# Attention and SwiGLU block on one core: order of batch 1, ends of the output tiles, and the place of the gate/value units changed

## The chip, the cores and the metric

The kernel runs on one core of one Trainium2 chip. The time is the device time of that core in microseconds (us); less is better. Three runs of the kernel before took 422.85, 424.26 and 424.94 us, so their median is 424.26 us.

## What is computed

Attention with 16 extra "beacon" keys, for 8 batches of 8 heads, 576 queries of 64 elements each, and then a SwiGLU block over all 4608 tokens, from 512 to 1536 and back to 512 columns:

```
B, H, S, Nb, D = (8, 8, 576, 16, 64)
k_all = np.concatenate([beacon_k, k], axis=2)
v_all = np.concatenate([beacon_v, v], axis=2)
scores = scale * np.matmul(q, k_all.transpose(0, 1, 3, 2))
causal[:, Nb:] = np.triu(np.ones((S, S), dtype=bool), k=1)
scores = np.where(causal, -1000000000.0, scores)
scores = scores - scores.max(-1, keepdims=True)
a = np.exp(scores)
a /= a.sum(-1, keepdims=True) + 1e-09
return np.matmul(a, v_all).astype(np.float32)
...
x = np.ascontiguousarray(attn_out.transpose(0, 2, 1, 3)).reshape(B * S, H * D)
...
g = x @ w_gate
silu = g * (1.0 / (1.0 + np.exp(-g)))
val = x @ w_val
return (silu * val @ w_out).astype(np.float32)
```

## The kernel before

The code writes out the order of every engine by hand (`manual_schedule`, line 83): each engine and each DMA queue runs its instructions in program order, and an instruction whose operand isn't ready holds all that stand behind it on its engine.

**Work pieces.** Attention is worked through in steps (b, m): batch b, pair of heads m = 0 to 3. A step has

- `scores1` and `scores2` (lines 245 to 249, by `scores`, line 210): matmuls of qT and kT into the PSUM tiles s_ps, two exponentials on ACT each, and selects for the causal mask on POOL; whatever loads wait in `pool_todo` are issued on POOL behind them;
- `pv` (line 253), once for each head of the pair *before*: 15 matmuls into pv_ps, a reciprocal and a multiply on DVE that write x.

The SwiGLU block runs over chunks of 512 tokens. Chunk j has 12 units `G()` (`gv_unit`, line 326): eight matmuls into gv_ps with the gate and value weights, a tanh on ACT, and two DVE operations (u, then hT). Its output is four tiles of 128 tokens; each takes 12 matmuls into o_ps, one for each unit of the chunk, then one DVE copy to o_sb and one DMA to the output on the queue of SP (`out_steps`, line 330). `F(n)` issues the next n of these output matmuls, so a call of `F` can end one tile and begin the next. Units wait in the list `gq`, output matmuls in `fq`; `G()` and `F(n)` do nothing where their list is empty.

**PSUM.** `big` holds three buffers of two banks that s_ps and gv_ps share in turn; `att` and `outp` are one bank each (lines 79 to 81). pv_ps sits in att. Output tiles of chunks 0 to 5 sit in outp alone (`one_bank`), as do the transposes of batch 1; later chunks alternate between outp and att (`two_banks`). So a new tile in outp waits until DVE has copied the tile before it.

**Where operands come from.** Batches 0 and 1 load q and k as fp32; `cast_k` (DVE) and `cast_q` (ACT for batch 1) make them bf16, and `transpose_k`, `transpose_q` turn one pair of heads on TensorE (five matmuls into outp, one DVE copy each). Batches 2 to 7 have q and k transposed by DMA: `dma_transposes(b)` (line 195) is a list of ten DMAs on the queue of SP, column blocks 0 to 4, k then q in each. `scores1` reads column blocks 0 to 4 of qT (the columns 112 to 575 in its second pair of matmuls). x is turned into xT by TensorE for batches 0 and 1 (`x_transpose_pair`, line 277) and by five or six DMAs on the queue of SP for later batches (`x_transpose`, line 285). The queue of SP therefore carries, in program order, the output DMAs, the transposes of q and k, and the transposes of x.

**The order around the change.** Lines 450 to 471 are batch 1: four steps with one unit of chunk 0 in each, then the rest. Lines 472 to 483 are a run of all 12 units of chunk 1, with one transpose of batch 2 behind each. Lines 486 to 517 are the main loop, steps (2,0) to (7,3), each of them

```
G()
scores1(b, m)
if prev:
    pv(*prev, 0)
F(n)
scores2(b, m)
G()
...
    pv(*prev, 1)
F(n)
```

followed by another `G()` and by up to four transposes of the next batch. Chunk b-1 is put into `gq` at the end of step (b,1), for b > 2; chunk b-2 into `fq` in the middle of step (b,1), for b > 3. Lines 518 to 538 are the tail: the last `pv`, the rest of chunk 6, chunks 7 and 8, and the last output tiles.

Of the kernel before, what the change touches and what calls it, by code (L numbers as in the profile page):

```python
# [36 lines left out]
def p_slice(t, q):  # L37

    if t == 0:
        return (0, 16 + q) if q < 496 else (1, 336 + q - 496)  # L40
    if t == 1:
        return 0, 512 + q - 112
    return 1, {2: -240, 3: 512 - 368, 4: 416 - 480}[t] + q
# [3 lines left out]
def kernel(  # L47
# [19 lines left out]
    NF = DFF // P  # L67
# [13 lines left out]
    outp = ctx.enter_context(tc.tile_pool(name="outp", bufs=1, space=bass.MemoryType.PSUM))  # L81
# [20 lines left out]
    def tiles(t):  # L102
        return t[:].rearrange("p (c h d) -> p c h d", c=NKT, h=H)
# [64 lines left out]
    def cast_k(b, m):  # L168
        d, t, h = tiles(kb[b % 2]), tiles(k32), slice(2 * m, 2 * m + 2)
        nc.vector.tensor_copy(d[:, 0:4, h, :], t[:, 0:4, h, :])  # L170
        return nc.vector.tensor_copy(d[0:80, 4, h, :], t[0:80, 4, h, :])

    def cast_q(b, m):
        d, t, h = tiles(qb[b % 2]), tiles(q32), slice(2 * m, 2 * m + 2)
        for o, i in ((d[:, 0:4, h, :], t[:, 0:4, h, :]), (d[0:64, 4, h, :], t[0:64, 4, h, :])):
            if b:
                nc.scalar.activation(o, i, ACT.Copy)
            else:
                nc.vector.tensor_copy(o, i)

    def transpose_pair(dst, src, n, b, m, pool, tag):
        t_ps = pool.tile([P, KPAD], BF16, name="t_ps", tag=tag)
        t, h = tiles(src[b % 2]), slice(2 * m, 2 * m + 2)
        for c in range(NKT):
            r = P if c < 4 else n
            nc.tensor.transpose(t_ps[:, P * c : P * c + r], t[0:r, c, h, :], ident[0:r, 0:r])  # L186
        nc.vector.tensor_copy(dst[b % 2][:, m, 0 : 4 * P + n], t_ps[:, 0 : 4 * P + n])  # L187

    def transpose_k(b, m, pool, tag):
        transpose_pair(kT, kb, 80, b, m, pool, tag)  # L190

    def transpose_q(b, m, pool, tag):
        transpose_pair(qT, qb, 64, b, m, pool, tag)
# [16 lines left out]
    def scores(b, m, which, spec, cols):  # L210
        s = [big.tile([P, 1024], FP32, name="s_ps", tag="big") for _ in range(2)]
        for t, col, q0, n in spec:
            for hh in range(2):
                r = slice(64 * hh, 64 * hh + 64)
                nc.tensor.matmul(  # L215
                    s[hh][:, col : col + n],
                    lhsT=kT[b % 2][r, m, P * t : P * t + P],
                    rhs=qT[b % 2][r, m, q0 : q0 + n],
                    start=True,
                    stop=True,  # L220
                )
        for hh in range(2):
            p = pt[2 * (m % 2) + hh][which]
            nc.scalar.activation(  # L224
                p[:, cols[0] : cols[1]], s[hh][:, cols[0] : cols[1]], ACT.Exp, scale=0.125
            )

            both = p[:].rearrange("p (a j) -> p a j", a=2)[:, :, 0:P]
            selects = [(both, [[0, 2], [1, P]], 0)]
            if which:  # L230
                selects.append((p[:, 416:512], [[1, 96]], -16))
            for ap, pattern, base in selects:
                nc.gpsimd.affine_select(  # L233
                    out=ap,
                    in_=ap,
                    compare_op=ALU.is_ge,
                    fill=0.0,
                    base=base,
                    pattern=pattern,
                    channel_multiplier=-1,  # L240
                )
        for load in pool_todo.pop(0) if pool_todo else []:
            load()
# [4 lines left out]
    def scores2(b, m):  # L248
        scores(b, m, 1, SCORES2, P2_COLS)
# [3 lines left out]
    def pv(b, m, hh):  # L253
        h = 2 * m + hh
        if h == 0:
            xs[b] = x_pool.tile([P, NKT, DM], BF16, name="x")
        o_ps = att.tile([P, NKT, 68], FP32, name="pv_ps", tag="att")
        for c, (q0, _) in enumerate(QBLOCKS):
            for t in range(c + 1):
                w, col = p_slice(t, q0)  # L260
                nc.tensor.matmul(  # L261
                    o_ps[:, c, 0 : D + 1],
                    lhsT=pt[2 * (m % 2) + hh][w][:, col : col + P],
                    rhs=vb[b % 2][:, t, h, 0 : D + 1],
                    start=(t == 0),
                    stop=(t == c),
                )
        rec = rec_pool.tile([P, NKT, 1], FP32, name="rec")
        nc.vector.reciprocal(rec[:], o_ps[:, :, D : D + 1])  # L269
        nc.vector.tensor_tensor(  # L270
            out=xs[b][:, :, D * h : D * h + D],
            in0=o_ps[:, :, 0:D],
            in1=rec[:].to_broadcast([P, NKT, D]),
            op=ALU.mult,
        )

    def x_transpose_pair(b, m, pool, tag):
        t_ps = pool.tile([P, S], BF16, name="xt_ps", tag=tag)
        for c, (q0, n) in enumerate(QBLOCKS):
            nc.tensor.transpose(  # L280
                t_ps[:, q0 : q0 + n], xs[b][0:n, c, P * m : P * m + P], ident[0:n, 0:n]
            )
        nc.vector.tensor_copy(xT[:, m, S * b : S * b + S], t_ps[:])
# [46 lines left out]
    def out_steps(j, pools):  # L330

        steps = []
        for i in range(TOK // P):
            st = {}

            def step(f, i=i, st=st):
                if f == 0:
                    pool, tag = pools[i % len(pools)]
                    st["o"] = pool.tile([P, DM], FP32, name="o_ps", tag=tag)
                nc.tensor.matmul(  # L340
                    st["o"][:],
                    lhsT=hTs[j][:, f, P * i : P * i + P],
                    rhs=wo[:, f, :],
                    start=(f == 0),
                    stop=(f == NF - 1),
                )
                if f == NF - 1:
                    o_sb = o_pool.tile([P, DM], FP32, name="o_sb")
                    nc.vector.tensor_copy(o_sb[:], st["o"][:])  # L349
                    r = TOK * j + P * i  # L350
                    nc.sync.dma_start(out[r : r + P, :], o_sb[:])

            steps += [lambda f=f, step=step: step(f) for f in range(NF)]
        return steps

    gq, fq = [], []
    one_bank = [(outp, "outp")]
    two_banks = [(outp, "outp"), (att, "att")]

    def G():  # L360
        if gq:
            return gv_unit(*gq.pop(0))

    def F(n):
        for _ in range(n):
            if fq:
                fq.pop(0)()
# [27 lines left out]
    last = NPAIR - 1  # L395
# [51 lines left out]
    G()  # L447


    for m in range(NPAIR):  # L450
        scores1(1, m)
        if m < last:
            cast_k(1, m + 1)
        if m >= 2:
            x_transpose_pair(1, m - 2, outp, "outp")
        if m:
            pv(1, m - 1, 0)
        scores2(1, m)
        if m < last:
            cast_q(1, m + 1)  # L460
            transpose_k(1, m + 1, outp, "outp")
        G()
        if m:
            pv(1, m - 1, 1)
        if m < last:
            transpose_q(1, m + 1, outp, "outp")
    x_transpose_pair(1, last - 1, outp, "outp")
    G()
    pv(1, last, 0)
# [7 lines left out]
    F(6)  # L477
    x_transpose_pair(1, last, att, "att")
    F(6)
    while gq:  # L480
        G()
        if todo:
            todo.pop(0)()

# [2 lines left out]
    prev = None  # L487
    for b in range(2, B):
        for m in range(NPAIR):
            n = 7 if b == 2 or (b, m) < (3, 2) else 6  # L490
            G()
            scores1(b, m)
            if prev:
                pv(*prev, 0)
            F(n)
            scores2(b, m)
            G()
            if m == 1 and b > 3:
                fq += out_steps(b - 2, one_bank)
            if prev:  # L500
                pv(*prev, 1)
            F(n)
            if m == 0 and b > 2:
                x_transpose(b - 1)
            if m == 1 and b > 2:
                gq += [(b - 1, f) for f in range(NF)]
            G()

            if m == 1 and b + 1 < B:
                todo = dma_transposes(b + 1)  # L510
                pool_todo += group(v_loads(b + 1, 0, H), 3)
            for _ in range(4):
                if todo:
                    todo.pop(0)()
            if m == 3 and b + 2 < B:
                pool_todo += group(k_loads(b + 2, 0, H) + q_loads(b + 2, 0, H), 6)
            prev = (b, m)
# [51 lines left out]
```

## Time and profile before

| | |
|---|---|
| median of three runs | 424.26 us (422.85 to 424.94) |
| the profiled execution | 422.26 us, its span in the profile 420.6 us |
| TensorE matmuls busy | 371.9 us (88% of the span) |
| DVE, ACT, POOL busy | 231.4, 171.6, 168.7 us |
| mean granted TensorE clock | 0.988 |

The profile's times are counted from the start of its span. "Busy" is the time in which an engine executes; the idle time of an engine is put down to the instruction that released it ("releaser"). A row of the timeline gives start, duration, engine, line, operation, its operands, and how many instructions were merged (x4); a bracket at its end is idle time of the engine just before it. "SPq" is the queue of SP, where DMAs are issued; the time from such an issue until its data has arrived is the time to landing. Landmarks of this execution: batch 1 begins at 43.5 us with its first scores, the run of chunk 1 at 82.6, step (2,0) at 103.45, the first unit of chunk 2 at 146.98, step (5,0) at 208.73, chunk 7 at 348.0, and the last output matmul ends at about 416.8 us.

### The profile page before, as it was taken

Reading aid. Unit: us, or ns where it says so; the run is one execution under the profiler, and the core shown is the slowest. Engines: PE = TensorE matmul, PEld = TensorE weight load, DVE = VectorE, ACT = ScalarE, POOL = GpSimd, SP = SyncE. Lnnn points to the kernel's source line nnn. Section 1 sums busy time; section 2 is a strip of 40 time slices with the busy share of each in tenths; the row PEclk is TensorE's granted clock in tenths of the full one; section 3 lists DMA queues with packets and bytes.
Section 4 is the critical chain, followed back from the end, with each engine's and each line's share of the span. In section 5 each row is a group of like instructions: output and inputs, shape, how many; then the busy total and the mean of one; then the engine's idle time right before and its main releaser. Section 6 shows DMA issues by size and latency. Waiting matters only on the chain.

```text
span 420.6 us, 7218 instructions
## 1 busy us (share of the span) xinstructions
PE 371.9 (88%) x2714; PEld 177.9 (42%) x2760; DVE 231.4 (55%) x446; ACT 171.6 (41%) x245; POOL 168.7 (40%) x328
## 2 busy tenths in 40 slices
PE   2787675899876698999999999999999999999996
PEld 1553343444342244444444444444444544444442
DVE  3647644578232236655555555555555565575561
ACT  1643654134553345545555555444555211232210
POOL 8682398720374835656193629261111100000000
PEclk9999989999998989999999999999999999999999
DMA  9999999993197999699499929991310031000012
GB/s 157 142 210 174 186 83 129 166 147 61 51 141 110 151 168 74 42 155 134 64 105 170 133 53 119 153 133 41 75 33 26 33 99 51 27 25 26 25 50 100
DMA packets 171746, 42.29 MB, mean 101 GB/s; under 512 B 161472, under 2 KB 167104, under 8 KB 171712
## 3 DMA queue, kind: packets, MB, share of 16 engines
q0 software_dynamic: 101664, 16.75, 54.8%
q1 hardware_dynamic: 67648, 24.49, 30.4%
q10 hardware_dynamic: 2400, 0.59, 0.7%
q8 instruction: 21, 0.34, 0.3%
q14 instruction: 13, 0.11, 0.1%
HBM read 38.27 MB, written 9.44 MB: 113 GB/s over the span
## 4 chain that ended last, share of the span: by engine, by line
PE 64%; DVE 14%; ACT 7%; DMA 5%; another core or an unknown queue 4%; issue 3%; SPq 2%; POOL 0%; DVEq 0%; ACTq 0%
PE gv_ps L305 32%; PE o_ps L340 18%; PE s_ps L215 7%; DVE u L319 5%; PE pv_ps L261 5%; DVE hT L322 5%; ACT th L317 4%; DMA xT<-x 3%; ACT p L224 2%; SPq L290 1%; DVE o_sb L349 1%; PE t_ps L186 1%; DVE x L270 1%; DMA k<-in_k_dram 1%
## 5 line engine op out<-in xcount | busy, mean ns | idle before, releaser
L319 DVE SCALAR_TENSOR_TENSOR u<-th,gv_ps 128x512 f32<-128x512 f32 x108 | 74.2, 687 | 120.6 <-ACT th L317 119.9
L317 ACT ACTIVATE th<-gv_ps 128x512 f32<-128x512 f32 x108 | 64.3, 597 | 176.9 <-PE gv_ps L305 152.2
L233 POOL TENSOR_SCALAR_AFFINE_SELECT p<-p 128x256 bf16<-128x256 bf16 x192 | 66.6, 381 | 154.8 <-ACT p L224 154.3
L224 ACT ACTIVATE p<-s_ps 128x720 bf16<-128x720 f32 (+1 forms) x128 | 103.3, 870 | 50.5 <-PE s_ps L215 50.5
L305 PE MATMUL gv_ps<-xT,wg 128*128 128x512 bf16 x416 | 112.1, 384 | 7.0 <-DMA xT<-x 2.5
L305 PE MATMUL gv_ps<-xT,wv 128*128 128x512 bf16 x424 | 110.8, 382 | 0.2
L340 PE MATMUL o_ps<-wo,hT 128*128 128x512 bf16 x410 | 102.7, 381 | 7.0 <-DVE o_sb L349 5.9
L322 DVE SCALAR_TENSOR_TENSOR hT<-gv_ps,u 128x512 bf16<-128x512 f32 x108 | 74.7, 691 | 3.7
L305 PEld LDWEIGHTS <-wv 128*128 128x128 bf16 x432 | 42.6, 99 | 52.8 <-issue 2.7
L305 PEld LDWEIGHTS <-wg 128*128 128x128 bf16 x432 | 40.6, 99 | 52.5 <-issue 7.7
L215 PE MATMUL s_ps<-qT,kT 64*128 64x96 bf16 (+5 forms) x384 | 45.3, 293 | 18.2 <-DVE qT L187 9.3
L340 PEld LDWEIGHTS <-hT 128*128 128x128 bf16 x432 | 39.4, 98 | 47.4 <-issue 7.9
L261 PEld LDWEIGHTS <-p 128*128 128x128 bf16 x960 | 35.6, 98 | 18.7 <-issue 9.8
L261 PE MATMUL pv_ps<-vb,p 128*128 128x65 bf16 x960 | 40.9, 195 | 0.9 <-DVE x L270 0.6
L114 POOL DMA_DIRECT2D vb<-in_v_dram x45 | 36.9, 838 | 0.0
L215 PEld LDWEIGHTS <-kT 64*128 64x128 bf16 x384 | 15.9, 96 | 49.0 <-issue 41.8
L349 DVE COPY o_sb<-o_ps 128x512 f32<-128x512 f32 x36 | 24.8, 688 | 15.0 <-PE o_ps L340 15.0
L270 DVE TENSOR_TENSOR x<-pv_ps,rec 128x320 bf16<-128x320 f32 x64 | 31.5, 492 | 2.2
L269 DVE RECIPROCAL rec<-pv_ps 128x5 f32<-128x5 f32 x64 | 12.0, 187 | 27.7 <-PE pv_ps L261 27.6
L114 POOL DMA_DIRECT2D kb<-in_k_dram x30 | 25.3, 864 | 2.3 <-DMA wo<-in_moe_w_out_dram 2.3
L114 POOL DMA_DIRECT2D qb<-in_q_dram x30 | 25.4, 886 | 0.0
L186 PE MATMUL t_ps<-ident,kb 128*128 128x128 bf16 (+1 forms) x40 | 4.7, 258 | 7.4 <-DVE kb L170 7.0
(30 smaller groups left out, 59.9 us busy)
## 6 DMA issues: line engine op xcount, KB each, us to landing
out_dram<-o_sb SPq DMA_DIRECT2D x36, 256.0 KB, 2.2
qb<-in_q_dram POOLq DMA_DIRECT2D x24, 128.0 KB, 5.8
vb<-in_v_dram POOLq DMA_DIRECT2D x21, 128.0 KB, 6.0
kb<-in_k_dram POOLq DMA_DIRECT2D x18, 128.0 KB, 4.4
k<-in_k_dram SPq DMA_DIRECT2D x16, 96.0 KB, 5.0
q<-in_q_dram SPq DMA_DIRECT2D x12, 128.0 KB, 6.5
wg<-in_moe_w_gate_dram POOLq DMA_DIRECT2D x4, 384.0 KB, 6.4
wv<-in_moe_w_val_dram POOLq DMA_DIRECT2D x4, 384.0 KB, 8.4
```

What stands on the lines that cost most here:

```text
L114: return eng.dma_start(dst[p0 : p0 + n, c, h0:h1, 0:D], src[b, h0:h1, r : r + n, :].rearrange("h j d -> j h d"))
L215: nc.tensor.matmul(s[hh][:, col : col + n], lhsT=kT[b % 2][r, m, P * t : P * t + P], rhs=qT[b % 2][r, m, q0 : q0 + n], start=True, stop=True,)
L224: nc.scalar.activation(p[:, cols[0] : cols[1]], s[hh][:, cols[0] : cols[1]], ACT.Exp, scale=0.125)
L233: nc.gpsimd.affine_select(out=ap, in_=ap, compare_op=ALU.is_ge, fill=0.0, base=base, pattern=pattern, channel_multiplier=-1,)
L261: nc.tensor.matmul(o_ps[:, c, 0 : D + 1], lhsT=pt[2 * (m % 2) + hh][w][:, col : col + P], rhs=vb[b % 2][:, t, h, 0 : D + 1], start=(t == 0 ...
L270: nc.vector.tensor_tensor(out=xs[b][:, :, D * h : D * h + D], in0=o_ps[:, :, 0:D], in1=rec[:].to_broadcast([P, NKT, D]), op=ALU.mult,)
L305: nc.tensor.matmul(gvs[f][:, TOK * half : TOK * half + TOK], lhsT=w[:, kk, P * f : P * f + P], rhs=xT[:, kk, r : r + TOK], start=(kk == 0) ...
L317: nc.scalar.activation(th[:], ps[:, 0:TOK], ACT.Tanh, scale=0.5)
L319: nc.vector.scalar_tensor_tensor(out=u[:], in0=th[:], scalar=1.0, in1=ps[:, 0:TOK], op0=ALU.add, op1=ALU.mult)
L322: nc.vector.scalar_tensor_tensor(out=hTs[j][:, f, :], in0=ps[:, TOK:1024], scalar=0.5, in1=u[:], op0=ALU.mult, op1=ALU.mult)
L340: nc.tensor.matmul(st["o"][:], lhsT=hTs[j][:, f, P * i : P * i + P], rhs=wo[:, f, :], start=(f == 0), stop=(f == NF - 1),)
L349: nc.vector.tensor_copy(o_sb[:], st["o"][:])
```

## The change

Four edits, all in the order of the work; every matmul, activation, copy and DMA stays.

- **Batch 1.** The casts of pair 1 move ahead of the loop, and those of pair m+2 into step m behind `scores2`. `transpose_k` of the next pair goes directly behind `scores1`, `transpose_q` behind the first `pv`, both ahead of `scores2`. `x_transpose_pair` of pair m-2 goes to the end of the step.
- **The run of chunk 1** takes in 12 output matmuls, six behind unit 5 and six behind unit 7. They are the second output tile of chunk 0, which stood in step (2,0).
- **F(6) everywhere in the main loop**, where the steps of batch 2 and the first two of batch 3 had F(7). A tile now begins in the first `F(6)` of a step and ends with the second.
- **Chunks enter the lists at the start of step (b,2)**, the units of chunk b-1 and (for b > 3) the output matmuls of chunk b-2. Both come one call later than before: the unit that stood at the end of step (b,1) now stands at the start of (b,2), and the output matmuls that began in the second `F` of (b,1) begin in the first `F` of (b,2).

```diff
+    cast_k(1, 1)
+    cast_q(1, 1)
     for m in range(NPAIR):
         scores1(1, m)
         if m < last:
-            cast_k(1, m + 1)
-        if m >= 2:
-            x_transpose_pair(1, m - 2, outp, "outp")
+            transpose_k(1, m + 1, outp, "outp")
         if m:
             pv(1, m - 1, 0)
+        if m < last:
+            transpose_q(1, m + 1, outp, "outp")
         scores2(1, m)
-        if m < last:
-            cast_q(1, m + 1)
-            transpose_k(1, m + 1, outp, "outp")
+        if m + 1 < last:
+            cast_k(1, m + 2)
+            cast_q(1, m + 2)
         G()
         if m:
             pv(1, m - 1, 1)
-        if m < last:
-            transpose_q(1, m + 1, outp, "outp")
+        if m >= 2:
+            x_transpose_pair(1, m - 2, outp, "outp")
...
-    while gq:
+    for i in range(NF):
         G()
+        if i in (5, 7):
+            F(6)
         if todo:
             todo.pop(0)()
...
     for b in range(2, B):
         for m in range(NPAIR):
-            n = 7 if b == 2 or (b, m) < (3, 2) else 6
+            if m == 2 and b > 2:
+                gq += [(b - 1, f) for f in range(NF)]
+                if b > 3:
+                    fq += out_steps(b - 2, one_bank)
             G()
             scores1(b, m)
             if prev:
                 pv(*prev, 0)
-            F(n)
+            F(6)
             scores2(b, m)
             G()
-            if m == 1 and b > 3:
-                fq += out_steps(b - 2, one_bank)
             if prev:
                 pv(*prev, 1)
-            F(n)
+            F(6)
             if m == 0 and b > 2:
                 x_transpose(b - 1)
-            if m == 1 and b > 2:
-                gq += [(b - 1, f) for f in range(NF)]
             G()
```

## The prediction, made before the changed kernel had run

> **What bounds the kernel now.** I read the page first, then the list of waits, then the timeline of the places that the diff touches.
>
> ```profile
> PE 371.9 (88%) x2714; PEld 177.9 (42%) x2760; DVE 231.4 (55%) x446; ACT 171.6 (41%) x245; POOL 168.7 (40%) x328
> PE s_ps L215 <- DVE qT L187: 9.3, 8, 2.3
> PE o_ps L340 <- DVE o_sb L349: 5.9, 7, 1.4
> PE s_ps L215 <- DMA qT<-qb: 2.8, 2, 2.0
> PE gv_ps L305 <- DMA xT<-x: 2.5, 2, 2.3
> ```
>
> TensorE is the bound, and the change takes no work from it. What can change is its idle time, and the waits say where that lies: on qT copied by DVE (batch 1), on o_sb (steps of batch 2 and 3), on DMA transposes. From 207 to 330 us the table by stage has PE busy 30.5 of 31 us; there is little to win and much to lose there.
>
> The queue of SP in batch 2, and at the edge from batch 4 to batch 5:
>
> ```profile
> 114.55 1.24 SPq L197 DMA_TRANSPOSE kT<-kb  x1
> 126.21 0.53 SPq L351 DMA_DIRECT2D out_dram<-o_sb  x1
> 128.15 1.19 SPq L197 DMA_TRANSPOSE qT<-qb  x1
> 130.69 0.57 PE L215 MATMUL s_ps<-qT,kT 64*128 64x464 bf16 x2 [0.76 <-DMA qT<-qb]
> 137.19 6.45 SPq L290 DMA_TRANSPOSE xT<-x  x5
> 146.98 1.58 PE L305 MATMUL gv_ps<-xT,wg 128*128 128x512 bf16 x4 [2.33 <-DMA xT<-x]
> ...
> 202.11 0.33 SPq L351 DMA_DIRECT2D out_dram<-o_sb  x1
> 203.90 1.20 SPq L197 DMA_TRANSPOSE qT<-qb  x1
> 205.81 0.49 DVE L270 TENSOR_TENSOR x<-pv_ps,rec 128x320 bf16<-128x320 f32 x1
> 208.73 1.04 PE L215 MATMUL s_ps<-qT,kT 64*128 64x496 bf16 x4
> ```
>
> In batch 2 the queue of SP is full from the first of batch 3's ten transposes (114.55) to the landing of the tenth (128.15 + 2.50 by the chain of waits, 130.65), and TensorE waits for it at 130.69. At the later edge the tenth is issued at 203.90 and lands 2.4 us later, 3 us before it is needed: this slack is what the change spends.
>
> [...]
> - [...] granted clock 0.50 in 53 to 55, 131 to 133 and 148 to 150 us, each about 3.4 us long and behind a stretch with about 2 us of idle.
> - [...] The output tiles here have one bank, and TensorE waits 0.78 us where the next tile follows at once.
> - [...] a transpose holds SP's queue 1.2 us and has landed after 2.3 to 2.5 us in quiet stretches, so ten in a row are bound by the queue.
>
> **Part by part.**
>
> *Batch 1, walked by hand with the durations of 43 to 79 us.* Step (1,0): the fp32 cast of pair 1 ends at 45.67 as before, so `transpose_k`, now ahead of `scores2`, waits for it from 44.1; its copy (0.47) frees outp, `transpose_q` goes at 46.7 and `scores2` at 47.2 instead of 45.20. But qT is ready at 47.9, and `scores1`(1,1) follows its unit at 49.45 instead of 50.45. In (1,1) the copy of kT stands on DVE behind u and hT of unit 6 (tanh behind four exponentials and the cast of q, which lands at 49.8): copied 52.7, `transpose_q` 52.8, `scores1`(1,2) 56.0 instead of 59.22. In (1,2) the same chain goes through x of the second `pv`: `scores1`(1,3) 63.1 instead of 66.78. Then `x_transpose_pair` of pairs 1 and 2 stand one behind the other on one bank and wait for DVE: unit 10 at 71.5 instead of 74.24, last `pv` 76.35 instead of 78.89. Gain 2.5. Bounds: the three waits for qT (2.01, 2.32, 2.32) gone whole, -6.7; their place taken whole by kT copies, 0, or +1.7 with a half-clock window in the 2.3 us hole at 69 to 71. I take -2.5.
>
> *Twelve output matmuls into the run of chunk 1*: 12 x 0.216 (four take 0.86 in the tail) = 2.6 us of TensorE come ahead of step (2,0) and leave the steps behind it. So (2,0) begins at 103.45 - 2.5 + 2.6 = 103.5. On SP the last three transposes of batch 2 now stand behind this tile's output DMA (98.1): tenth issued 101.2, landed 103.5, needed at 104.0. Cost 0, with 0.5 us of cover.
>
> *Tile ends in batches 2 and 3.* The o_sb waits there (0.78, 0.78, 1.41, 0.78, 0.78, 0.98 = 5.5 us) go, since a unit's place, scores and a `pv` now cover each copy. What is late next is SP. Batch 3's first transpose stands behind the tile ending with step (2,1): 103.5 + 8.7 of steps, + 0.16 + 0.69 copy + 0.45 output issue = 113.55, against 114.55. From there the queue is full again, 16.1 us to the tenth landing: 129.65, against 130.65. TensorE has done its work at about 121.4 and stands idle, so all but 1.0 of the gain is lost. Then the transposes of x(2): x is ready 1.9 us earlier (135.3), but now an output DMA stands ahead of them, whose tile ends later (`F`, 135.8; copy and issue to 137.0). They start at 137.1 instead of 137.19, and the first unit of chunk 2 waits for the fourth as before: about 146.9 instead of 146.98. POOL, whose load issues hold the selects to 138 us, lies inside this wait. Everything up to here: 0. If it isn't absorbed, -2.6.
>
> *Batch edges 5, 6, 7.* In the main loop tiles ended with the first `F(6)`; now with the second, half a step later. The tenth transpose stands behind the second tile of step (b-1,3). For b = 5: `F` ends 205.18, but o_sb stands on DVE behind hT and x (to 206.30), so copied 207.02, output issued to 207.38, ninth transpose 207.47, tenth 207.47 + 1.27 + 0.10 = 208.84, landed 208.84 + 2.35 = 211.2. The second pair of `scores1`(5,0) ran at 209.4 (the first waits for a buffer until 209.20). Stall 1.8, with nothing on TensorE's queue that could pass it: `pv`, `F`, `scores2` all stand behind. The same distances hold at b = 6 (tenth issued 244.9, scores 249.83) and b = 7 (286.42, 290.92). At b = 4 no outputs run and SP is ahead. 3 x 1.8 = +5.4. Bounds: 0 if it lands 2 us sooner than I think; 3 x 2.4 with DMAs less quiet.
>
> *Tail.* Before, the last tile of chunk 5 ended behind unit 10 of chunk 6, with unit 11 after it:
>
> ```profile
> 342.78 0.69 DVE L322 SCALAR_TENSOR_TENSOR hT<-gv_ps,u 128x512 bf16<-128x512 f32 x1
> 343.39 0.68 DVE L349 COPY o_sb<-o_ps 128x512 f32<-128x512 f32 x1
> 344.12 4.04 PE L340 MATMUL o_ps<-wo,hT 128*128 128x512 bf16 x17 [0.36 <-DVE o_sb L349]
> ```
>
> Now all units stand one call later, three output matmuls follow each of the last four, and the tile ends behind unit 11, directly ahead of the 18 matmuls that begin a tile in the same bank. Its copy stands behind u and hT of unit 11: 0.2 + 0.60 + 0.72 + 0.72 + 0.68 = 2.95 after the unit, less 0.65 for the three matmuls: stall 2.3, less the 0.5 of before, +1.8; a smaller one of 0.2 at the tile begun behind unit 8. +2.0. Bounds +1.0 and +3.6 (a half-clock window more).
>
> *Chunks one call later*: the units' number and order are the same. Unit 0 of chunk 3 has 1.73 us more for its xT (0.2 us waited at 184.63): -0.2. At b = 5 xT is issued 1.15 later, behind an output, and needed 1.73 later: 0.
>
> **Sum.** 0 + 5.4 + 2.0 - 0.2 = +7.2 us on the span: the profiled execution of 422.26 (span 420.6) becomes 429.5. The median of the runs shown lies 2.0 higher than that execution, so I carry the difference over: 424.26 + 7.2 = 431.5.
>
> **Rivals.** No change is told from a change here below 0.5%, about 2.1 us (422.1 to 426.4).
> 1. *The gain of batch 1 survives* past SP's queue in batch 2, since less output traffic shortens it: +4.6, 428.9. For it: the landings there scatter from 2.4 to 6.1 us. Against: ten issues in a row take the time, not the landings.
> 2. *The edges stay covered*: only the tail's 2.0 is left, 426.3. It needs the tenth landing by 209.4, 1.8 us sooner; then the queue's order would have to be other than the program's, and the trace has no such case.
> 3. *Faster*, by one mechanism: SP's queue keeps ahead of TensorE at all edges, in batch 2 as well, because the transposes are issued as soon as q and k have been loaded. Then the o_sb waits up to step (3,0) (3.75) and the 2.5 of batch 1 are won, the tail lost: -4.3, 420.0. It decides from a start of batch 3's transposes at 107 us or sooner. Against: they start 0.45 us behind the output's issue at 114.1 in this trace though the last of their sources, issued by 87, had landed 8.7 later, by 96.
> 4. *Half clock*: the new stalls of about 2 us (three edges, the tail, the 7 us in batch 2) put two windows of 3.4 us at half clock, 1.7 us each: +10.6, 434.9. Of the six places with about 2 us of idle in this trace three were followed by one.
>
> **How the numbers follow.** The forecast 0.58 (428 to 434 by its own bounds), rival 1 0.12, rival 2 0.10, rival 3 0.08, rival 4 0.12. Range 426 to 435.5: it leaves out rival 3 and some of rivals 2 and 4. Faster 0.08 (rival 3); same 0.09 (most of rival 2); slower 0.83.
>
> **What would show it.** In the list of waits o_sb falls from 5.9 to about 2.7 us, now in the tail, and qT from DMA rises from 2.8 to about 7 + 3 x 1.8 = 12. The first scores of batches 5, 6, 7 carry an idle time of about 1.8 released by a DMA of qT; the first unit of chunk 2 stands near 147. If those scores have no such idle time, the main term is wrong; if step (3,0) begins before 125, the batch 2 term is.

## The result, and the profile after

The changed kernel takes 437.14 us (median of 4 runs, 436.13 to 439.1), the kernel before beside it 424.6 us (4 runs): ratio 1.029, 95% interval 1.0213 to 1.0366. The forecast was 431.5 us with a range of 426 to 435.5: the direction is right, the size is not. The profiled execution of the changed kernel took 436.66 us; its span is 435.0 us and its mean granted clock 0.961 (before: 420.6 and 0.988). The ratios leave out runs more than 1.5% above the fastest of the same kernel (nine of 20 in experiment 4), so they can differ from the quotient of two medians in the third decimal.

The page's busy line of the changed kernel, and then its list of waits (in total, times, longest):

```profile
PE 380.1 (87%) x2760; PEld 179.7 (41%) x2760; DVE 230.2 (53%) x446; ACT 171.9 (40%) x245; POOL 168.6 (39%) x328
```

```profile
PE s_ps L215 <- DMA qT<-qb: 12.7, 5, 5.5
PE gv_ps L305 <- DMA xT<-x: 6.8, 1, 6.8
...
PE s_ps L215 <- DVE qT L187: 2.3, 4, 0.6
PE o_ps L340 <- DVE o_sb L349: 2.1, 1, 2.1
```

The forecast named two of these numbers: about 12 us for qT from DMA and about 2.7 for o_sb. Both came, at 12.7 and 2.1. DVE's copies of qT cost 7 us less than before. The page also has TensorE *busy* 8 us longer with the same work, but that comparison isn't clean: 46 of 2760 matmul records are missing from the trace of before (x2714), and a second profile of the kernel before, with all 2760, has 381.0 us (experiment 9). That some of the loss is no waiting at all, which the list of waits can't show, is seen in single rows below.

The timeline of the changed kernel at the places that the forecast walked through: batch 2, the edge to batch 5, and the tail.

```profile
116.80 1.23 SPq L197 DMA_TRANSPOSE kT<-kb  x1
122.05 0.53 SPq L351 DMA_DIRECT2D out_dram<-o_sb  x1
130.30 1.19 SPq L197 DMA_TRANSPOSE qT<-qb  x1
134.16 0.57 PE L215 MATMUL s_ps<-qT,kT 64*128 64x464 bf16 x2 [2.81 <-DMA qT<-qb]
141.94 6.81 SPq L290 DMA_TRANSPOSE xT<-x  x5
153.39 1.86 PE L305 MATMUL gv_ps<-xT,wg 128*128 128x512 bf16 x4 [6.84 <-DMA xT<-x]
...
209.99 0.33 SPq L351 DMA_DIRECT2D out_dram<-o_sb  x1
211.71 1.20 SPq L197 DMA_TRANSPOSE qT<-qb  x1
214.12 0.37 PE L215 MATMUL s_ps<-qT,kT 64*128 64x464 bf16 x2 [1.49 <-DMA qT<-qb]
214.89 1.46 PE L340 MATMUL o_ps<-wo,hT 128*128 128x512 bf16 x6
...
356.11 0.68 DVE L349 COPY o_sb<-o_ps 128x512 f32<-128x512 f32 x1
356.84 5.73 PE L340 MATMUL o_ps<-wo,hT 128*128 128x512 bf16 x18 [2.08 <-DVE o_sb L349]
```

In batch 2 the queue of SP is full from 116.80 to 131.49, TensorE waits for the tenth transpose and then for xT. At the edge an output DMA at 209.99 stands ahead of the last two transposes, and scores stall 1.49 us; the edges to batches 6 and 7 show 1.43 and 1.42. In the tail 18 matmuls wait 2.08 us for the copy ahead of them. They then take 5.73 us, where 17 of them took 4.04 before: half clock (granted 0.50 from 357.27 to 360.68 us). The first unit of chunk 2 stands at 153.39 us, where the forecast had 147.

### The profile page after: what moved, and what is told of

The parts are those of the page before. It is cut to its first block, busy times and chain, and to the rows that moved or that the text cites. A ratio compares the mean times of both kernels' runs of the same rounds, so it can differ in the third digit from the quotient of the medians.

```text
span 435.0 us, 7257 instructions
## 1 busy us (share of the span) xinstructions
PE 380.1 (87%) x2760; PEld 179.7 (41%) x2760; DVE 230.2 (53%) x446; ACT 171.9 (40%) x245; POOL 168.6 (39%) x328
## 4 chain that ended last, share of the span: by engine, by line
PE 63%; DVE 10%; DMA 10%; SPq 5%; ACT 5%; POOL 3%; issue 3%; ACTq 0%; DVEq 0%; POOLq 0%
PE gv_ps L305 32%; PE o_ps L340 20%; PE s_ps L215 5%; PE pv_ps L261 5%; DMA q<-in_q_dram 4%; DVE u L319 4%; DVE hT L322 4%; ACT th L317 3%; DMA qT<-qb 2%; SPq L197 2%; DMA xT<-x 2%; ACT p L224 1%; SPq L108 1%; DMA k<-in_beacon_k_dram 1%; POOL qb L114 1%
## 5 line engine op out<-in xcount | busy, mean ns | idle before, releaser
L305 PE MATMUL gv_ps<-xT,wg 128*128 128x512 bf16 x432 | 114.2, 386 | 9.5 <-DMA xT<-x 6.8
L305 PE MATMUL gv_ps<-xT,wv 128*128 128x512 bf16 x432 | 113.2, 384 | 0.0
L340 PE MATMUL o_ps<-wo,hT 128*128 128x512 bf16 x432 | 107.8, 387 | 2.1 <-DVE o_sb L349 2.1
L215 PE MATMUL s_ps<-qT,kT 64*128 64x80 bf16 (+5 forms) x384 | 46.5, 305 | 18.8 <-DMA qT<-qb 12.7
L261 PE MATMUL pv_ps<-vb,p 128*128 128x65 bf16 x960 | 42.2, 197 | 5.4 <-DVE x L270 4.0
L261 PEld LDWEIGHTS <-p 128*128 128x128 bf16 x960 | 36.6, 100 | 23.6 <-issue 10.8
```

The costliest lines, as they stand in the source:

```text
L215: nc.tensor.matmul(s[hh][:, col : col + n], lhsT=kT[b % 2][r, m, P * t : P * t + P], rhs=qT[b % 2][r, m, q0 : q0 + n], start=True, stop=True,)
L261: nc.tensor.matmul(o_ps[:, c, 0 : D + 1], lhsT=pt[2 * (m % 2) + hh][w][:, col : col + P], rhs=vb[b % 2][:, t, h, 0 : D + 1], start=(t == 0 ...
L305: nc.tensor.matmul(gvs[f][:, TOK * half : TOK * half + TOK], lhsT=w[:, kk, P * f : P * f + P], rhs=xT[:, kk, r : r + TOK], start=(kk == 0) ...
L340: nc.tensor.matmul(st["o"][:], lhsT=hTs[j][:, f, P * i : P * i + P], rhs=wo[:, f, :], start=(f == 0), stop=(f == NF - 1),)
```

## Experiments

The kernel before was timed beside every group of runs: medians 427.17 us (39 runs, 423.88 to 432.94), 428.6 (23), 425.45 (11) and 427.51 (11). The three runs that the forecast started from lay at 424.26, and the profiled one at 422.26. This matters below. Ratios are to the kernel before in the same group. Most runs ask whether the queue of SP does what the forecast said; the others ask where the gain of batch 1 went.

**1. The output matmuls back at their old place** (the units stay one call late), in the main loop of the changed kernel:

```diff
                 gq += [(b - 1, f) for f in range(NF)]
-                if b > 3:
-                    fq += out_steps(b - 2, one_bank)
...
             G()
+            if m == 1 and b > 3:
+                fq += out_steps(b - 2, one_bank)
```

> The changed kernel with one thing undone: chunk b-2 enters the list of output matmuls in the middle of step (b,1) again, so tiles of chunks 2 to 5 end with the first F(6) of a step; the units stay half a batch late. Theory Q (the queue of SP decides at the batch edges, the single bank of the output tiles in the tail): the idle time before the second pair of scores of batches 5, 6 and 7 (1.49, 1.43, 1.42 in the changed kernel) is gone, and the 2.08 us wait for o_sb before the 18 output matmuls too, with the half-clock window behind it: 3 x 1.67 + 1.7 + 1.7 = 8.4 us less than the changed kernel, near 428.5. Rival U (the late units do it, since they meet the scores in another place): the stalls stay, 435 to 438.

Measured 425.55 us (20 runs), ratio 0.9976 (0.9952 to 1.0000); span of its profile 423.8. The timeline of this run at the edge to batch 5:

```profile
204.16 0.33 SPq L351 DMA_DIRECT2D out_dram<-o_sb  x1
206.42 1.20 SPq L197 DMA_TRANSPOSE qT<-qb  x1
210.79 1.03 PE L215 MATMUL s_ps<-qT,kT 64*128 64x496 bf16 x4
```

The output DMA leaves early enough, the tenth transpose is issued 4.4 us ahead of the scores (in the changed kernel 0.1 us), and the four matmuls run without a stall. The place of the output matmuls alone makes the edges and the tail late. It costs about 12 us between medians of different groups (437.14 and 439.13 against 425.55), and 9.2 us in the profiles from chunk 2 to chunk 7: more than the 7.4 that the forecast had for them.

**2. The transposes ahead of the second tile's end** at the edges, the rest as changed:

```diff
+            if m == 1 and b + 1 < B:
+                todo = dma_transposes(b + 1)
+            for _ in range(4):
+                if b > 3 and todo:
+                    todo.pop(0)()
             F(6)
...
             if m == 1 and b + 1 < B:
-                todo = dma_transposes(b + 1)
...
             for _ in range(4):
-                if todo:
+                if b <= 3 and todo:
                     todo.pop(0)()
```

> The changed kernel, but from batch 4 on the four transposes of a step are issued ahead of its second F(6) instead of behind it; nothing else moves, tiles end with the second F(6) as in the changed kernel. Theory Q: the tenth transpose no longer stands behind the output DMA of its own step, lands some 5 us sooner, and the three waits at the edges are gone: 5.0 us less than the changed kernel, near 432; the tail keeps its wait of 2.1 us. Rival U (the place of units and tiles on TensorE and DVE makes the stall): no change, 436 to 438.

Measured 430.38 us, ratio 1.0103 (1.0009 to 1.0197). Its timeline:

```profile
201.09 1.23 SPq L197 DMA_TRANSPOSE qT<-qb  x1
209.60 0.33 SPq L351 DMA_DIRECT2D out_dram<-o_sb  x1
211.40 1.03 PE L215 MATMUL s_ps<-qT,kT 64*128 64x496 bf16 x4
...
351.58 4.05 PE L340 MATMUL o_ps<-wo,hT 128*128 128x512 bf16 x17 [2.08 <-DVE o_sb L349]
```

The same output DMA leaves at about the same time, now behind the transposes, whose tenth was issued at 201.09, and the scores don't stall. So at the edges it is the order in the queue of SP, not load on the DMA engines. The tail's stall is untouched.

**3. Batch 1 in its old order**, the other edits kept (the diff of batch 1 reversed).

> The changed kernel with the order of batch 1 as it was before; all else as in the changed kernel. Theory H (the new order of batch 1 saves the waits I walked, 2.5 us, and loses as much to one more window at half clock): the same time as the changed kernel within 1.5 us, with one half-clock window in batch 1 in place of two. Rival W (the new order is a gain that something else hides): 2.5 us slower than the changed kernel, 439.5. Rival W2 (the new order is itself the loss): 2 us or more faster, below 435.

Measured 441.74 us, ratio 1.035 (1.0257 to 1.0442). In the first profile batch 1 had gained nothing: from its first scores to the first tanh of chunk 1 it took 41.04 us before and 41.12 after. This run takes 45.12 us for the stretch. That favours theory W: the new order is a gain of 2.6 to 4.6 us between medians (437.14 and 439.13 of the changed kernel), which the comparison of two single executions had hidden. The intervals of the ratios overlap, so this run alone doesn't settle it; experiment 5 does.

**4. Batch 3's transposes in the run of chunk 1**, two per unit, so that batch 2 has none:

```diff
-    todo = dma_transposes(2)
+    todo = dma_transposes(2) + dma_transposes(3)
...
-        if todo:
-            todo.pop(0)()
+        for _ in range(2):
+            if todo:
+                todo.pop(0)()
...
-                todo = dma_transposes(b + 1)
+                todo = dma_transposes(b + 1) if b > 2 else []
```

> The changed kernel, but the ten transposes of batch 3 are issued in the run of chunk 1, right behind those of batch 2 (two for each unit), instead of in steps (2,1) to (2,3). Theory Q for batch 2: the 5.5 + 2.8 us of idle before the scores of step (3,0) are gone, and with them the half-clock stretch from 128 to 139 us; step (3,0) begins at about 125, xT(2) is issued about 10 us sooner, the first unit of chunk 2 stands at 142 to 144 instead of 153.4: 9 to 12 us less than the changed kernel, 425 to 428. Rival D (the wait for xT and the loads on POOL decide there, not the queue of SP): step (3,0) begins sooner, but the first unit of chunk 2 stands at 150 or later: 434 to 437.

Measured 428.58 us (20 runs), ratio 1.0013 (0.9978 to 1.0048), 0.6 us above what was expected. The timeline, first of the queue of SP, then of TensorE:

```profile
120.38 10.04 SPq L351 DMA_DIRECT2D out_dram<-o_sb  x3
130.48 6.72 SPq L290 DMA_TRANSPOSE xT<-x  x5
...
124.63 0.58 PE L215 MATMUL s_ps<-qT,kT 64*128 64x496 bf16 x4
...
142.11 1.87 PE L305 MATMUL gv_ps<-xT,wg 128*128 128x512 bf16 x4 [5.07 <-DMA xT<-x]
```

Step (3,0) begins at 124.63 without a stall (130.75 in the changed kernel), and the first unit of chunk 2 comes 11.3 us sooner. What is left is the wait for xT. SP's queue was the bound of batch 2 up to step (3,0).

**5 to 7. One edit at a time, on the kernel before**: the new batch 1 alone; the chunks entering both lists at the start of step (b,2) alone; the tile ends (`F(6)` everywhere and 12 output matmuls in the run) alone. Each diff is that part of the change. Then the changed kernel once more.

> The kernel before with the new order of batch 1 and nothing else of the change. Theory W (the new order saves about what I walked, 2.5 us, and the half-clock windows that the kernel before meets in batch 1 fall differently from run to run): 2 to 4 us faster than the kernel before in the median, ratio 0.990 to 0.995; from the first scores of batch 1 to the first tanh of chunk 1 about 41.0 us in every run. Theory H (the saved waits are lost again to half-clock windows): ratio 0.998 to 1.003. Rival: the loss of the whole change comes from here, ratio above 1.005.

> The kernel before with the chunks entering the lists at the start of step (b,2), units and output matmuls, and nothing else of the change (F(7) in the early steps stays). Theory Q: the tiles of chunks 2 to 5 end with the second F of a step, so the tenth transpose of batches 5, 6, 7 lands late (3 x 1.67 us), and in the tail the 18 output matmuls wait for o_sb (1.7, with a half-clock window behind it 3.4): 6.7 to 8.4 us slower than the kernel before, ratio 1.016 to 1.020. Rival U2 (these stalls are absorbed when batch 2 isn't late as well): ratio below 1.005.

> The kernel before with 12 output matmuls in the run of chunk 1 and F(6) in every step of the main loop, and nothing else of the change. Theory Q for batch 2: TensorE reaches step (3,0) 4 us sooner, waits there longer for the same queue of SP, goes through two or three half-clock windows for it, and xT(2) stands behind an output DMA: the first unit of chunk 2 is reached 3 to 6 us later than in the kernel before, ratio 1.007 to 1.014. Rival (the tile ends gain the 5.5 us of waits for o_sb): ratio 0.987 to 0.995.

> The changed kernel once more, on the chip of the other three, to compare with them: ratio 1.02 to 1.037 as measured first, and a granted clock near 0.96 in each run. If the parts add up, its loss is the sum of those of the other three kernels of this call.

| kernel | us, median | ratio to the kernel before | interval |
|---|---|---|---|
| batch 1 alone | 423.37 | 0.9896 | 0.9826 to 0.9967 |
| chunks late alone | 438.66 | 1.0245 | 1.0185 to 1.0305 |
| tile ends alone (20 runs) | 429.96 | 1.0051 | 1.0022 to 1.0079 |
| the changed kernel again | 439.13 | 1.0239 | 1.0165 to 1.0313 |

The parts add up to 1.9%, within the interval of the whole. One part carries the loss. Each part missed its expectation a little: batch 1 gained more (5.2 us against 2 to 4), the late chunks cost more (2.45% against 1.6 to 2.0) and the tile ends less (0.5% against 0.7 to 1.4). The tile ends move a wait, as the list of waits of that run shows beside the one of before (5.9 for o_sb, 2.8 for qT, 2.5 for xT):

```profile
PE gv_ps L305 <- DMA xT<-x: 7.1, 1, 7.1
PE s_ps L215 <- DMA qT<-qb: 6.8, 2, 5.4
...
PE o_ps L340 <- DVE o_sb L349: 0.4, 1, 0.4
```

5.5 us of waits for o_sb went, and 8.6 us of waits for DMAs came.

**8. The first hole of batch 1 filled**: 28 transposes behind its first scores, whose results nothing reads.

```diff
         scores1(1, m)
+        if m == 0:
+            fill = outp.tile([P, KPAD], BF16, name="fill", tag="outp")
+            kt = tiles(kb[1])
+            for i in range(28):
+                c = i % 4
+                nc.tensor.transpose(fill[:, P * c : P * c + P], kt[:, c, 0:2, :], ident[:])
```

> The changed kernel, with 28 more transposes on TensorE behind the first scores of batch 1, whose results nothing reads: they fill the 1.8 us in which it waits for the cast of k. Theory H (that hole is what puts the next 6.8 us at half clock): no half-clock window from 46 to 53 us any more, and from the first scores of batch 1 to the first tanh of chunk 1 38.5 to 39.5 us in place of 41.0. Rival (the waits in batch 1 set its length, the clock only rides along): 41 us as before, or more.

The total doesn't decide (436.34 us, ratio 1.0254, 1.0186 to 1.0323). The timeline does, first of the changed kernel, then of this one:

```profile
46.43 0.59 PE L186 MATMUL t_ps<-ident,kb 128*128 128x128 bf16 x5 [1.79 <-DVE kb L170]
48.86 1.89 PE L305 MATMUL gv_ps<-xT,wg 128*128 128x512 bf16 x4
```

```profile
45.15 1.74 PE L459 MATMUL fill<-ident,kb 128*128 128x128 bf16 x28
47.18 0.55 PE L186 MATMUL t_ps<-ident,kb 128*128 128x128 bf16 x5 [0.29 <-DVE kb L170]
49.05 1.04 PE L305 MATMUL gv_ps<-xT,wg 128*128 128x512 bf16 x4
```

With work that nobody needs in the 1.79 us of idle, the unit behind it runs at full clock (1.04 us in place of 1.89 for the same four matmuls; granted clock 1.00 from 45 to 54 us in place of 0.62), and the stretch of batch 1 falls from 41.12 to 38.87 us. One execution doesn't show that the filling did it: in experiment 10 the same hole, unfilled (1.96 us), was followed by a unit of 1.04 us too. This execution has one half-clock window in the stretch, as the profiled execution of before had with 41.04: with one window each, and its first hole filled, the new order takes 2.2 us less.

**9. The kernel before, unchanged, profiled a second time.**

> The kernel before, unchanged, profiled a second time. Theory L (the first profiled execution, 422.26 us with three half-clock windows at a granted clock of 0.988, was the luckiest kind; the 39 timed ones had 0.960 to 0.988): now the span is 423 to 430 us at a clock of 0.965 to 0.982, and the stretch from the first scores of batch 1 to the end of its units (41.04 us there) is 42 to 45.5 us with two to four windows. Rival F (the windows stand where the program puts them): the same three windows behind 51, 130 and 147 us, 41.0 us for the stretch, span 420 to 422.

Median 427.44 us (10 runs). In the profile the span is 427.2 us, the clock 0.975, and the stretch of batch 1 takes 45.52 us with four windows (granted 0.78 from 51 to 82 us): theory L. The page's row of the granted clock (tenths, 40 slices of the span), for the first profile of the kernel before, this one, and the changed kernel:

```profile
PEclk9999989999998989999999999999999999999999
```

```profile
PEclk9999978899998989999999999999999999999999
```

```profile
PEclk9999698999996869999999999999999999999999
```

The stretches side by side, from landmarks in the three traces (us; a tanh of unit 0 marks a chunk's start):

| stretch | before, first | before, second | changed |
|---|---|---|---|
| start to the first scores of batch 1 | 43.52 | 45.18 | 44.05 |
| from there to chunk 1 (batch 1) | 41.04 | 45.52 | 41.12 |
| chunk 1 to chunk 2 (batch 2) | 65.74 | 66.59 | 71.83 |
| chunk 2 to chunk 6 (edges) | 159.54 | 159.20 | 162.49 |
| chunk 6 to chunk 7 (tail) | 40.09 | 40.09 | 44.84 |
| chunk 7 to the end | 70.62 | 70.62 | 70.62 |

Against the first profile batch 1 gains nothing and batch 2 loses 6.1 us. Against the second, batch 1 gains 4.4 and batch 2 loses 5.2. The difference in span is 14.4 us against the first and 7.8 against the second.

**10 and 11. The parts that help, put together.** First: the new batch 1, the tile ends, batch 3's transposes early (the edit of 4), and both lists filled where the kernel before fills them. Second: the same, and x of batch 2 is turned by TensorE:

```diff
             scores1(b, m)
+            if (2, 2) <= (b, m) <= (3, 1):
+                x_transpose_pair(2, 4 * b + m - 10, outp, "outp")
...
-            if m == 0 and b > 2:
+            if m == 0 and b > 3:
                 x_transpose(b - 1)
```

> What the other kernels point to, together: the new order of batch 1, the 12 output matmuls in the run of chunk 1 and F(6), but the chunks enter the lists where they did before, and batch 3's transposes are issued in the run of chunk 1. From the kernel with batch 3's transposes early (426.5 us span) the waits at three edges with their half-clock windows (3 x 3.5) and the tail (1.8) go: near 414 us, ratio to the kernel before 0.965 to 0.975 by theory Q. If the place of the units matters for something else, above 0.985.

> The repaired kernel with x of batch 2 turned by TensorE (four groups of five transposes and a copy, as in batches 0 and 1) in place of five DMAs on the queue of SP. Theory Q: the first unit of chunk 2 no longer waits for the DMA; it follows step (3,1) at about 135 instead of 143, 5 to 8 us less than the repaired kernel, ratio near 0.955. Rival (the loads on POOL hold the selects of step (3,0), and so this place, whatever xT does): 2 us or less.

Measured 417.11 us, ratio 0.9808 (0.9764 to 0.9853), and 413.9 us, ratio 0.9733 (0.9688 to 0.9779). Both beat both kernels; both gain less than expected. For the second step the timeline shows why:

```profile
132.08 0.42 PE L280 MATMUL xt_ps<-ident,x 112*128 112x112 bf16 x5 [0.27 <-DVE o_sb L349]
...
134.07 0.54 PE L261 MATMUL pv_ps<-vb,p 128*128 128x65 bf16 x10 [1.43 <-POOL p L233]
...
139.57 1.03 PE L305 MATMUL gv_ps<-xT,wg 128*128 128x512 bf16 x4
```

The wait of 5.0 us for xT is gone, and chunk 2's first unit follows step (3,1) without one. But four pairs of 0.42 us and four waits of 0.27 for the bank are new (2.8 us), and the wait for POOL's selects in step (3,1), 2.84 us in the first of the two kernels, is still 1.43. 5.0 - 2.8 + 1.4 = 3.6, and the first tanh of chunk 2 comes 3.5 us sooner (its first matmul 1.9: in the first kernel a half-clock window falls on the first units of chunk 2, in the second on the matmuls ahead of them). The first kernel's profiled span, 414.8 us, is close to the sum of its expectation (426.5 - 10.5 - 1.8 = 414.2); its ratio fell short at least in part because in that group the kernel before was itself at its fastest, 425.45. The rest wasn't followed up.

## Why the prediction was wrong

The mechanisms of its sum held, and most of its terms too. The step that failed in the difference between the kernels is the half clock, put at 0; the base that the difference was added to was too low as well. Step by step:

- **Batch 1, -2.5.** Right on average, in part by luck, since the walk has no half clock in it. With one window each and the first hole filled the gain is 2.2 us (experiment 8). Five profiled executions with the old order took 41.0 to 41.1 us with one window and 45.1 to 45.5 with four; the eight with the new order and no filling took 40.6 to 41.3 with one to three. The means are 43.6 and 41.0 us.
- **Twelve output matmuls in the run, cost 0.** Right: from chunk 1 to step (2,0) took 18.89 us before and 21.48 after, which is the 2.6 us of work, and at step (2,0) no stall of note followed.
- **Tile ends, "everything up to here: 0".** The mechanism is right. Batch 3's first transpose is issued 10.15 us after step (2,0) began (10.05 forecast), SP's queue is the bound and takes what the o_sb waits gave. The size depends on the execution that one compares with: from the first scores of batch 1 to chunk 2 the change costs 6.2 us against the first profile, 0.8 against the second. All profiles with the same order up to there have 106.8, 112.1 and 112.2 us in the old one and 110.8 to 113.0 (four) in the new one; the means differ by 1.6. What the walk left out is seen in the chain of waits of the changed kernel (start, duration, what):

```profile
141.55 0.33 SPq L351
...
141.94 1.37 SPq L290
...
146.09 7.16 DMA xT<-x
...
153.39 3.57 PE gv_ps L305 x8
```

  The output ahead of xT leaves at 141.55, as forecast in kind but 4.9 us later in time: in that execution batch 1 began 0.5 us later and took 2.6 longer than walked, and the ten transposes took 1.2 more to the last landing. The fourth piece of xT landed after 7.16 us (5.76 before). TensorE ran the six output matmuls at half clock there (the chain has 2.56 us for them at 135.67).
- **Edges, 3 x 1.8.** Right: 41.10 us from step (5,0) to step (6,0) before, 42.76 after, so 1.66 each. Experiments 1 and 2 show the cause.
- **Tail, +2.0.** Right: in experiment 2 the stretch from chunk 6 to chunk 7 is 43.15 against 40.09. Of the 3.06, 1.3 are six output matmuls that now fall into it, and 1.76 is the stall. (The walk's five durations add up to 2.92, not 2.95, and the wait of before is 0.36 in the line that it shows, not 0.5: small beside the term.)
- **Half clock. This is the step that failed.** The forecast took 0 for it, and kept it as rival 4 with two windows of 1.7 us for 0.12. Its own count, three of six places with about 2 us of idle followed by a window, spoke for about two windows behind four new stalls. Six profiled executions have the edge stalls (two of the changed kernel, and experiments 3, 4, 6 and 8). Of their 18 edges 11 were followed by a window at half clock, of the seven that have the tail's stall (experiment 2 as well) 2. From step (6,0) to (7,0) it takes 44.26 to 44.31 us with a window and 42.69 to 42.71 without, so 1.6 each: 3 x 11/18 x 1.6 + 2/7 x 1.6 = 3.4 us as an estimate (from step (5,0) to (6,0) a window cost more, 1.9 to 2.7 us). The late chunks alone (experiment 6) point the same way: 2.45% is some 10 us, against 7.2 forecast for edges, tail and xT. The second profile of the changed kernel, with 437.1 us of span, has all three edges followed by one:

```profile
212.53 0.37 PE L215 MATMUL s_ps<-qT,kT 64*128 64x464 bf16 x2 [1.49 <-DMA qT<-qb]
213.30 2.59 PE L340 MATMUL o_ps<-wo,hT 128*128 128x512 bf16 x6
```

  The same six matmuls behind the same stall took 1.46 us in the first profile. This time isn't in the stall, but in the row behind it.
- **The base.** It failed too, in the time itself and not in the difference: "The median of the runs shown lies 2.0 higher than that execution, so I carry the difference over". Three runs and one profile of the kernel before stood at the low end of its spread. The medians of its later groups lie between 425.45 and 428.6, those with most runs at 427.2 and 428.6, so 3 to 4 us above 424.26. In the first group, with four runs, the kernel before lay only 0.3 above it. The same error sits in the parts: what the edits in batches 1 and 2 are worth was measured from an execution with three half-clock windows where the second profile had six.

Put together from the measured terms: 0.8 up to chunk 2, 3 x 1.66 at the edges, 1.76 in the tail, 3.4 of half clock, less 0.4 seen elsewhere between chunks 2 and 6 (3.3 us measured there + 1.3 us of matmuls moved out = 4.6, against 5.0) make +10.5 us, of which 3.4 are the half clock; without it the sum is 7.1, beside the 7.2 forecast. Measured between medians: 12.5 and 10.5 us. That the sum meets one of these exactly is chance, since the 0.8 rests on one pair of executions. All eight runs of the changed kernel have a median of 438.3 us, the 94 later ones of the kernel before 427.3. So of the 6.8 us between 438.3 and the forecast of 431.5 the base makes 3.0 and the difference between the kernels 3.8.

The rivals: the gain of batch 1 doesn't survive batch 2 (rival 1), the edges aren't covered (rival 2), SP's queue isn't ahead (rival 3; step (3,0) would have begun before 125, it began at 130.75). Rival 4, 434.9 us, was nearest; its difference of 10.6 us is about the one measured.

## What to carry to other kernels

Here a stall of TensorE of 1.4 to 1.5 us that ended in half clock cost about twice its length (1.6 us more from step (6,0) to (7,0)), so where a change opens a new one of that size, price the half clock with it, and look behind the stall, not only at it. Profile the kernel before twice before anything is compared with a single execution of it, and look at the row of the granted clock first: where it differs between two executions of the same program, a difference of that size between two kernels isn't yet the effect of an edit. Where one queue carries outputs and operands, a tile's end that moves by half a step can cost more than all waits that it removes.

## What the runs showed that was not expected

**Like stalls were followed by half clock in one place and by full clock in another.** The first profiles of the two kernels have these stretches at a granted clock of 0.50 between 40 and 400 us, each set beside TensorE's idle time in the 3.41 us ahead of it:

| kernel | granted 0.50 from, us | for, us | TensorE idle in the 3.41 us ahead, us |
|---|---|---|---|
| before | 51.73 | 3.41 | 2.01 |
| before | 130.24 | 3.41 | 2.33 |
| before | 147.30 | 3.41 | 2.33 |
| changed | 46.66 | 6.83 | 1.89 |
| changed | 67.14 | 3.41 | 1.77 |
| changed | 128.57 | 10.24 | 3.32 |
| changed | 149.06 | 10.24 | 2.50 |
| changed | 357.27 | 3.41 | 2.08 |

Counted in windows of 3.41 us, the shortest of them, the stretches are one, two or three windows long, and in both executions their starts lie whole multiples of 3.413 us apart (23 and 5 times in the first). The length of a stall alone doesn't tell what follows. In the kernel before a wait of 2.01 us for qT, over at 50.45, was followed by half clock from 51.73; the waits of 2.32 us that were over at 59.22 and 66.78 were followed by full clock (1.00 from 55.14 to 130.24). In the changed kernel the same stall of 1.49 us at the edge to batch 5 was followed by full clock in the first profile (1.00 from 159.30 to 357.27 us) and by half clock in the second (0.52 from 213.5 to 217). What decides between the two isn't shown.

One program takes 422 to 433 us. In the 94 later timed runs of the kernel before the medians are 425.2 us at a granted clock of 0.98 and more (37 runs), 428.1 from 0.975 (33), 429.0 from 0.97 (16) and 430.8 below (8). Against such a spread the profile of a single execution can hide a gain of 4 us.

**A row of DMA transposes cost here what its issues took.** In the first profiles of the two kernels the ten transposes of q and k of a batch hold SP's queue for 12.3 to 14.0 us in sum (twelve rows of ten), and the scores of step (3,0), which wait for the tenth, stood idle 2.81 us for it in the changed kernel. Moving those of batch 3 into the run of chunk 1, where TensorE doesn't wait for them (experiment 4), gave some 10 us against the changed kernel (428.58 against 437.14 and 439.13).
